# Transposing the probability tiles of two more head pairs by DMA, in attention followed by two feed-forward layers

## The chip, the cores and the metric

The kernel runs on one core of a Trainium2 chip. Its engines are TensorE (PE; its weight loads are listed apart as PEld), VectorE (DVE), ScalarE (ACT), GpSimd (POOL) and SyncE (SP), which here only issues DMAs. The metric is the device time of one execution in microseconds (us).

## What is computed

Attention over 4 batches, 8 heads, 576 positions and 64 channels, with a cut: scores more than tau (0.02) below their row's maximum are dropped. Two feed-forward layers follow on the 2304 tokens.

```
scores = q @ k.T / sqrt(64)
scores = where(scores >= max(scores) - tau, scores, -1e9)
attn = exp(scores - max(scores)); attn /= sum(attn) + 1e-9
x = attn @ v                                   # 2304 x 512
h = ((x @ w1) * (x @ w2)) @ w3 @ w_out         # 1024 wide, back to 512
g = elu(h @ w_in)                              # 2048 wide
out = g @ w_out2                               # 2304 x 512
```

All matmuls keep float32 accuracy. Most operands are split into a high and a low float32r part, and a product is three matmuls (high by high, high by low, low by high).

## The kernel before

**Attention.** The 32 heads are 16 pairs (`NPAIR`); a pair has nine tiles of 128 query rows by 576 keys, so there are 144 tiles, numbered i in the order of `SEQ`. Pairs 0 to 3 ("plain", `NPL = 4`) use unsplit float32 queries and keys. Pairs 4 to 15 use split ones: POOL scales the queries of a head by 1/8 (`prep_s`, L313), ACT makes the high part (`prep_h`, L326), POOL makes the low parts (`prep_lq`, `prep_lk`, L330 and L334).

The path of a tile: PE computes the scores S into a PSUM tile of two banks, of which there are three (`emit_S`, L394 or L406). DVE takes the negated row maximum (`emit_max`, L415). POOL makes a bias for the exponential (`emit_bias`, L423; only for plain tiles and those that a DMA transposes) and then the threshold (`emit_tiny`, L419). ACT takes the exponential (`emit_exp`, L428 or L430). DVE cuts it at the threshold and sums the rows (`emit_mask`, L436). Then P has to be turned so that the keys lie on partitions, in one of two ways:

- On PE: five transposes into the tile's own PSUM banks (`emit_X`, L484) and an ACT copy out of them (`emit_C`, L488). The product with V is then in float32 (`emit_PV`, L541). The PSUM tile stays taken until the copy is done.
- By DMA: ACT rounds P to float16 (`emit_H`, L443), POOL makes the rest that the rounding left (`emit_L`, L447 for 512 columns and L448 for 64), and SP issues a DMA transpose of both (`emit_T`, L474 or L476). The product with V is in float16 (L549). H and L go into a ring of four buffers `hl`, which a DMA transpose frees; the PSUM tile is free after the mask.

Which way a tile goes is said by `of_dma(p, n)`, where n = 0 are the first four tiles of a pair and n = 1 the other five. Before, the n = 0 tiles go by DMA from pair 10 on and the n = 1 tiles from pair 4 on (and of pairs 1 and 3). V in float16 needs a scale for each pair (`v_sum`, `v_mean`, `v_scale`, `prep_v`, `prep_vl`); it is made for every pair from 4 on.

The reciprocals of the row sums of a group (p, n) are made by DVE (`emit_rr`, L496), turned by a PE transpose into unused columns of the PSUM tile of a later score tile (`turn_r`, L502), copied by ACT, stored to DRAM and loaded again as a broadcast. The group's PV waits for that load, and DVE multiplies by it (`emit_xf`).

**First layer, part one.** For a batch of four pairs, both branches x·w1 and x·w2 are computed in units of 8 feature blocks by 2 branches by 2 token groups (`run_ab`, L591; evicted at L599 and L606, and stored to DRAM as g). The units of batches 0 to 2 are planned among the attention tiles, those of batch 3 follow them.

**The planner.** Everything so far is a list of `Op`s with an engine, a duration, dependences and a due time (`key`, mostly the tile number plus a few tiles). `Plan.run` goes through a model of the engines and emits, at each step, among the ops that can begin within `SLACK` of the earliest on an engine, that with the lowest key. `AHEAD` moves the keys by the name of the function and a stage. The result is a fixed instruction order on each engine; nothing is decided on the chip.

**Part two and the second layer** are ordered by hand. w3·w_out is multiplied out first: eight units of 24 matmuls (`m_unit`, L922) into four PSUM banks, each evicted by ACT and DVE (L931, L932) three units later. Among them the next weights are unpacked (L252 to L277: ACT, DVE, DVE, DVE, ACT, POOL for a chunk), and the first block of g is loaded and split (`load_g` L986, `split_g` L241 and L242). Then x2 = M·g (L1125), and the second layer (L1115 to L1280), whose output matmuls (L1206) fill PE to the end.

Of the kernel before, what the change touches and what calls it, by code (L numbers as in the profile page):

```python
# [50 lines left out]
SLACK = {"PE": 0, "DVE": 0.08, "ACT": 0.03, "POOL": 0.27, "SP": 0.09, "NEW": 0.05}  # L51
AHEAD = {
    ("emit_C", 0): 101, ("emit_C", 1): -80.5, ("emit_C", 2): 21, ("emit_H", 1): -14, ("emit_H", 2): 69.5,
    ("emit_L", 2): -5, ("emit_S", 0): 69, ("emit_S", 2): -3.5, ("emit_T", 1): -130, ("emit_T", 2): -16,
    ("emit_X", 0): 3.5, ("emit_X", 2): -0.5, ("emit_bias", 0): 11, ("emit_bias", 1): -33.5, ("emit_bias", 2): -3,
    ("emit_exp", 0): -27.5, ("emit_exp", 1): -18, ("emit_exp", 2): 54.5, ("emit_mask", 0): -37,
    ("emit_mask", 1): -95, ("emit_mask", 2): -18, ("emit_max", 0): -1.5, ("emit_max", 1): -26.5,
    ("emit_max", 2): 17.5, ("emit_rr", 0): -7, ("emit_rr", 1): 36.5, ("emit_tiny", 0): 8, ("emit_tiny", 1): 4,
    ("emit_tiny", 2): -49, ("emit_xf", 0): -88.5, ("emit_xf", 1): -91, ("emit_xh", 0): -44.5, ("emit_xh", 1): 60,
    ("emit_xl", 0): -66.5, ("emit_xl", 1): -29.5, ("evict_a", 0): -25.5, ("evict_a", 1): -24, ("evict_a", 2): 122.5,  # L60
    ("evict_g", 0): -29, ("evict_g", 1): -52, ("evict_g", 2): -1, ("high", 0): -62, ("join", 0): -28.5,
    ("keep_busy", 0): -64, ("keep_r", 0): -22.5, ("keep_r", 1): -20, ("load_plain", 0): 13.5, ("load_qk", 0): 95.5,
    ("load_rs", 0): 39, ("load_rs", 1): 2, ("load_v", 0): 34, ("load_w", 0): -48.5, ("low", 0): 13.5,
    ("new_pt", 0): -58, ("prep_h", 0): -240.5, ("prep_lk", 0): 67, ("prep_lq", 0): -13, ("prep_v", 0): 74,
    ("prep_vl", 0): 21, ("rest", 0): 0.5, ("run_ab", 1): 3, ("run_ab", 2): -4, ("sign", 0): 32.5,
    ("store_g", 0): -98, ("store_g", 1): 93, ("store_g", 2): -149, ("store_r", 0): -12.5, ("store_r", 1): 7,
    ("top", 0): 82, ("turn_r", 0): -155.5, ("turn_r", 1): -142, ("v_mean", 0): -4, ("v_scale", 0): -187,
    ("v_sum", 0): 140.5,
# [8 lines left out]
class Op:  # L77
    def __init__(self, fn, eng, us, key, kb, land, port):
        self.fn, self.eng, self.us, self.key, self.kb, self.land, self.port = fn, eng, us, key, kb, land, port
        self.deps, self.outs, self.n, self.at = [], [], 0, 0.0  # L80
        self.gets = self.frees = None


class Plan:
# [48 lines left out]
    def run(self):  # L133
# [11 lines left out]
        for _ in self.ops:  # L145
# [39 lines left out]
def attention_moe_moe2(  # L185
# [126 lines left out]
    def prep_s(h):  # L312
        G.tensor_scalar(raw[h][:, :S], raw[h][:, :S], esc, 0.0, op0=ALU.mult, op1=ALU.add)  # L313
# [62 lines left out]
    def of_dma(p, n):  # L376
        return p >= 10 if n == 0 else p >= NPL or p % 2 == 1
# [47 lines left out]
    def emit_exp(i):
        et[i] = ep.tile([P, 2, HS], F32, tag="e", name=f"e{i}")
        if i < NPL * TPP:
            A.activation(et[i], sc[i][:, :, :HS], AF.Exp, bias=st[i][:, 2:3], scale=esc)  # L428
        else:
            A.activation(et[i], sc[i][:, :, :HS], AF.Exp, bias=st[i][:, 2:3] if by_dma(i) else st[i][:, 0:1])  # L430

    def emit_mask(i):
        p, pos = SEQ[i]
        if pos == 0:
# [206 lines left out]
    for i in range(NTILE + 4):  # L641
        p, pos = SEQ[i] if i < NTILE else (NPAIR - 1, 0)
        d = 0.02 if i >= NTILE else 1.08 if p < NPL else 1.1 if pos == 8 else 0.58
# [4 lines left out]
        mx = MAX[i] = op(call(emit_max, i), [o], "DVE", 0.672, i)  # L648
# [5 lines left out]
        bi = op(call(emit_bias, i), [mx], "POOL", 0.22, i - 10) if plain or by_dma(i) else mx  # L654
        ty = op(call(emit_tiny, i), [mx, bi], "POOL", 0.24, i - 9)
# [721 lines left out]
```

## Time and profile before

| | us |
|---|---|
| median of three runs | 1008.46 |
| lowest and highest | 1004.95, 1008.83 |
| the profiled execution: its own time | 1006.17 |
| the profiled execution: from first to last instruction | 1004.4 |
| TensorE busy in it | 964.4 (96%) |

The stretches of the profiled execution, in us from its first instruction: attention with tiles 0 to 71 up to about 196, pairs 8 and 9 (tiles 72 to 89) to about 241, pairs 10 to 15 to about 415, the branches of batch 3 to 470, w3·w_out to 518, x2 to 623, the second layer to the end. The chain that ended last can be followed back to 578 us, and nearly all of it is TensorE.

In the windows view a line is a stretch: its length, then for each engine the busy time and the number of instructions, the granted TensorE clock (1.00 is 2.4 GHz, 0.50 is 1.2 GHz), the mean busy share of the 16 DMA engines, and GB/s.

### The profile page before, as it was taken

Reading aid. Unit: us, or ns where it says so; the run is one execution under the profiler, and the core shown is the slowest. Engines: PE = TensorE matmul, PEld = TensorE weight load, DVE = VectorE, ACT = ScalarE, POOL = GpSimd, SP = SyncE. Lnnn points to the kernel's source line nnn. Section 1 sums busy time; section 2 is a strip of 40 time slices with the busy share of each in tenths; the row PEclk is TensorE's granted clock in tenths of the full one; section 3 lists DMA queues with packets and bytes.
Section 4 is the critical chain, followed back from the end, with each engine's and each line's share of the span. In section 5 each row is a group of like instructions: output and inputs, shape, how many; then the busy total and the mean of one; then the engine's idle time right before and its main releaser. Section 6 shows DMA issues by size and latency. Waiting matters only on the chain. (4 is left out here: it accounts for less than half of the span.)

```text
span 1004.4 us, 18071 instructions
## 1 busy us (share of the span) xinstructions
PE 964.4 (96%) x6102; PEld 846.7 (84%) x6102; DVE 716.5 (71%) x1234; ACT 564.2 (56%) x1045; POOL 657.6 (65%) x849
## 2 busy tenths in 40 slices
PE   8899999989999999999999999999999999999998
PEld 5556788858888888899789999898989999899997
DVE  7887988868776677489775654789676656765563
ACT  5787778768666566355435334645555344553442
POOL 4468787868898999255322223888787576875662
PEclk9999999979999999999999999999999999999999
DMA  8446666577887967777747965731215221141201
GB/s 270 152 127 194 135 147 160 143 163 156 190 185 176 191 159 150 192 259 252 250 152 246 311 228 173 260 116 54 65 51 180 72 69 52 49 132 58 69 22 63
DMA packets 182263, 152.51 MB, mean 152 GB/s; under 512 B 119484, under 2 KB 168860, under 8 KB 177564
## 3 DMA queue, kind: packets, MB, share of 16 engines
q1 hardware_dynamic: 178060, 121.72, 44.8%
q10 hardware_dynamic: 4112, 29.66, 8.4%
q8 instruction: 48, 0.79, 0.3%
q14 instruction: 43, 0.35, 0.1%
HBM read 98.89 MB, written 24.72 MB: 123 GB/s over the span
## 5 line engine op out<-in xcount | busy, mean ns | idle before, releaser
L591 PE MATMUL ab<-x,W 128*128 128x256 f32 (+1 forms) x1536 | 227.4, 298 | 0.8 <-DVE xf L560 0.7
L1206 PE MATMUL o<-W,gg 128*128 128x512 f32 x864 | 222.9, 390 | 0.0
L591 PEld LDWEIGHTS ab<-x,W 128*128 128x128 f32 x1536 | 208.3, 188 | 8.2 <-issue 5.2
L1115 POOL TENSOR_TENSOR wi<-wr,wi 128x256 fp32r<-128x256 f32 x168 | 144.3, 871 | 65.8 <-ACT wi L1114 53.3
L1206 PEld LDWEIGHTS o<-W,gg 128*128 128x128 f32 x864 | 159.9, 188 | 21.5
L436 DVE SCALAR_TENSOR_TENSOR e<-s,st,e 128x576 f32<-128x576 f32 x144 | 115.7, 813 | 31.3 <-ACT e L430 24.8
L1194 POOL TENSOR_TENSOR gg<-th,gg 128x384 fp32r<-128x384 f32 x96 | 106.3, 1108 | 46.5 <-PE h L1246 26.4
L415 DVE TENSOR_REDUCE st<-s 128x1 f32<-128x576 f32 x144 | 107.0, 751 | 27.4 <-PE s L406 12.7
L447 POOL TENSOR_TENSOR hl<-e,hl 128x512 f16<-128x512 f32 x94 | 110.4, 1175 | 19.7 <-ACT hl L443 19.2
L1246 PE MATMUL h<-sl,wi 128*128 128x384 f32 x576 | 116.5, 338 | 2.1 <-DVE th L1276 1.2
L1188 ACT ACTIVATE et<-et 128x384 f32<-128x384 f32 x96 | 50.1, 522 | 111.9 <-DVE et L1187 111.5
L1246 PEld LDWEIGHTS h<-sl,wi 128*128 128x128 f32 x576 | 102.5, 188 | 11.2 <-DVE th L1276 2.0
L1125 PE MATMUL x<-sl,M 128*128 128x384 f32 x576 | 100.6, 336 | 1.4 <-DVE sl L242 1.4
L1125 PEld LDWEIGHTS x<-sl,M 128*128 128x128 f32 x576 | 99.8, 188 | 2.1 <-DVE sl L242 2.0
L1193 ACT ACTIVATE gg<-th 128x384 fp32r<-128x384 f32 x96 | 50.6, 527 | 76.9 <-DVE th L1191 76.5
L1276 DVE TENSOR_TENSOR th<-h,th 128x384 f32<-128x384 f32 x96 | 53.2, 554 | 56.9 <-PE h L1246 56.8
L406 PE MATMUL s<-qk 128*128 128x288 f32 x480 | 86.7, 310 | 7.1 <-DVE e L436 3.7
L430 ACT ACTIVATE e<-s,st 128x576 f32<-128x576 f32 x108 | 77.8, 736 | 27.1 <-POOL st L423 21.5
L1246 PE MATMUL h<-so,wi 128*128 128x384 f32 x432 | 87.5, 337 | 2.6 <-ACT th L1286 1.8
L1246 PEld LDWEIGHTS h<-so,wi 128*128 128x128 f32 x432 | 76.6, 188 | 10.8 <-ACT th L1286 3.9
L406 PEld LDWEIGHTS s<-qk 128*128 128x128 f32 x480 | 69.5, 192 | 17.0 <-issue 6.2
L1191 DVE SCALAR_TENSOR_TENSOR th<-et,th 128x384 f32<-128x384 f32 x96 | 71.6, 746 | 16.8 <-ACT et L1188 15.4
(112 smaller groups left out, 1539.0 us busy)
## 6 DMA issues: line engine op xcount, KB each, us to landing
wr<-wi_dr SPq DMA_DIRECT2D x168, 128.0 KB
rqk<-in_qk SPq DMA_DIRECT2D x24, 576.0 KB
raw_wo<-in_wo ACTq DMA_DIRECT2D x12, 1024.0 KB
th<-g_dr SPq DMA_DIRECT2D x48, 192.0 KB
raw_w<-in_w SPq DMA_DIRECT2D x8, 1024.0 KB
raw_w<-in_w3t ACTq DMA_DIRECT2D x8, 1024.0 KB
raw_win<-in_win ACTq DMA_DIRECT2D x8, 1024.0 KB
vr<-in_v SPq DMA_DIRECT2D x16, 320.0 KB
```

The lines of the kernel that those rows point to most:

```text
L406: T.matmul(s[:, n, :HS], q, k[:, c:c + HS], start=(x == 0), stop=(x == len(ops) - 1))
L415: V.tensor_reduce(st[i][:, 0:1], sc[i][:, :, :HS], axis=AX.XY, op=ALU.max, negate=True)
L430: A.activation(et[i], sc[i][:, :, :HS], AF.Exp, bias=st[i][:, 2:3] if by_dma(i) else st[i][:, 0:1])
L436: V.scalar_tensor_tensor(et[i], sc[i][:, :, :HS], st[i][:, 1:2], et[i], op0=ALU.is_ge, op1=ALU.mult, accum_out=sm[p][:, pos:pos + 1],)
L447: G.tensor_tensor(t[:, S + 64:], e[:, :512], t[:, :512], op=ALU.subtract)
L591: T.matmul(o[:, :w], wf[:, m, wx, kt, :], x[:, xx, :], start=(kt == 0 and k == 0), stop=(kt == NK - 1 and k == 2),)
L1115: G.tensor_tensor(t[:, 1], r, f32(t[:, 0]), op=ALU.subtract)
L1125: T.matmul(o[:, :TB], M[:, f, mx, e * P:(e + 1) * P], gh[j, f][:, gx, :], start=(k == 0), stop=(k == 23),)
L1191: V.scalar_tensor_tensor(x, c["t"], -1.0, x, op0=ALU.add, op1=ALU.max)
L1194: G.tensor_tensor(h[:, 1, :], x, f32(h[:, 0, :]), op=ALU.subtract)
L1206: T.matmul(po[j, t], dst["h"][:, gx, t * P:(t + 1) * P], WO[f][:, wx, :], start=(first and k == 0), stop=(last and k == 2),)
L1246: T.matmul(o[:, :TB], w[:, wx, kt, :], bs[k][:, kt, xx, :], start=(i == 0), stop=(i == 5),)
```

## The change

- `of_dma`: the n = 0 tiles go by DMA from pair 8 on. These are eight tiles, four each of pairs 8 and 9.
- Scores of pairs 4 to 15 are computed negated (`prep_s` multiplies by `nesc`), the row maximum becomes a minimum, and the mask compares with `is_le`. Thereby threshold and bias are both a sum with the same minimum, and one POOL instruction writes them side by side (`emit_tiny`); `emit_bias` is left for plain tiles alone.
- `turn_r` uses the PSUM tile of q + 3, not q + 2.
- In the stage of w3·w_out, `load_g` is issued after the first four units, two at a time, and `split_g` starts after the fourth unit, not after the first.
- The planner: new durations, new `SLACK`, a rule that PE's writes into a PSUM tile and the other engines' reads of it don't overlap (`bank`, `wr`), and an `AHEAD` of 377 entries, by groups of twelve tiles or two pairs, where there were 74. The order on every engine is thus new up to 470 us.

```diff
-SLACK = {"PE": 0, "DVE": 0.08, "ACT": 0.03, "POOL": 0.27, "SP": 0.09, "NEW": 0.05}
+SLACK = {"PE": 0.0, "DVE": 0.07, "ACT": 0.06, "POOL": 0.35, "SP": 0.0, "NEW": 0.05}
...
+        if o.bank in self.touched[not o.wr]:
+            t = max(t, self.touched[not o.wr][o.bank] + LAT)
...
+            if o.bank is not None:
+                self.touched[o.wr][o.bank] = end
...
     def prep_s(h):
-        G.tensor_scalar(raw[h][:, :S], raw[h][:, :S], esc, 0.0, op0=ALU.mult, op1=ALU.add)
+        G.tensor_scalar(raw[h][:, :S], raw[h][:, :S], nesc, 0.0, op0=ALU.mult, op1=ALU.add)
...
     def of_dma(p, n):
-        return p >= 10 if n == 0 else p >= NPL or p % 2 == 1
+        return p >= 8 if n == 0 else p >= NPL or p % 2 == 1
...
+        plain = SEQ[i][0] < NPL
-        V.tensor_reduce(st[i][:, 0:1], sc[i][:, :, :HS], axis=AX.XY, op=ALU.max, negate=True)
+        V.tensor_reduce(st[i][:, 0:1], sc[i][:, :, :HS], axis=AX.XY, op=ALU.max if plain else ALU.min, negate=plain)
...
     def emit_tiny(i):
         t = st[i]
-        G.tensor_scalar(t[:, 1:2], t[:, 0:1], -1.0, add2[:, (k := int(i >= NPL * TPP)):k + 1], op0=ALU.mult, op1=ALU.add)
+        if SEQ[i][0] < NPL:
+            G.tensor_scalar(t[:, 1:2], t[:, 0:1], -1.0, add2, op0=ALU.mult, op1=ALU.add)
+            return
+        w = 1 + by_dma(i)
+        G.tensor_tensor(t[:, 1:1 + w], lift[:, :w], t[:, 0:1].to_broadcast([P, w]), op=ALU.add)
...
-        i = q + 2
+        i = q + 3
-        tr = op(call(turn_r, p, n, i), [r, S_[i]], "PE", 0.11, q)
+        tr = op(call(turn_r, p, n, i), [r, S_[i]], "PE", 0.08, q, bank=i, wr=True)
...
+    def next_g(f):
+        split_g(0, f)
+        load_g(JS[1], f)
+
-    for f in range(NF1):
-        load_g(JS[0], f)
     for f in range(NF1):
         while jobs and f not in w3s:
             run_jobs(1)
         run_unit(m_unit(f), 2)
+        if f < 4:
+            load_g(JS[0], 2 * f)
+            load_g(JS[0], 2 * f + 1)
         if f < 6:
             run_jobs(4)
-        split_g(0, f)
-        load_g(JS[1], f)
+        if f > 2:
+            next_g(f - 3)
+    for f in range(NF1 - 3, NF1):
+        next_g(f)
     flush(0)
```

## Rows read from the trace of the kernel before

**Rows 1.** The page: busy us and share of the span of each engine.

```profile
PE 964.4 (96%) x6102; PEld 846.7 (84%) x6102; DVE 716.5 (71%) x1234; ACT 564.2 (56%) x1045; POOL 657.6 (65%) x849
```

**Rows 2.** The windows view, by stretches (columns as told above).

```profile
0.00:196.00 196.00, 184.91 (x1398) 138.06 (x1399) 164.70 (x337) 145.92 (x230) 137.79 (x232) 1.00 0.61 168
196.00:241.00 45.00, 40.71 (x284) 31.52 (x285) 34.33 (x75) 32.11 (x55) 33.30 (x53) 0.89 0.66 151
241.00:415.00 174.00, 163.45 (x1374) 150.69 (x1369) 123.03 (x272) 112.72 (x199) 148.89 (x260) 1.00 0.81 174
250.00:350.00 100.00, 94.03 (x762) 86.17 (x761) 69.94 (x155) 64.29 (x113) 87.20 (x149) 1.00 0.85 187
470.40:518.36 47.96, 45.47 (x195) 37.11 (x194) 39.02 (x36) 20.11 (x28) 17.11 (x7) 0.96 0.64 226
623.00:1004.40 381.40, 373.28 (x1860) 334.43 (x1859) 253.46 (x396) 182.07 (x413) 267.61 (x270) 1.00 0.28 89
```

**Rows 3.** Waits of PE, whole span: total us, times, longest.

```profile
PE s L502 <- DVE st L415: 5.2, 7, 1.7
...
PE m L922 <- DVE M L932: 2.5, 1, 2.5
...
PE s L502 <- DVE rr L497: 2.1, 3, 0.9
```

**Rows 4.** Timeline of SP at 202 us: start, us, what.

```profile
202.47 6.19 SPq L476 DMA_TRANSPOSE pt<-hl  x4
```

**Rows 5.** Timeline of ACT there; in brackets the idle time before, and its releaser.

```profile
207.00 0.68 ACT L443 ACTIVATE hl<-e 128x576 f16<-128x576 f32 x1 [2.13 <-DMA pt<-hl]
```

**Rows 6.** Timeline of PE there.

```profile
201.88 0.77 PE L484 MATMUL s<-ident,e 128*128 128x128 f32 x5
202.58 1.08 PE L541 MATMUL pv<-pt,vr 128*64 128x256 f32 x8
...
208.33 2.82 PE L406 MATMUL s<-qk 128*128 128x288 f32 x12 [1.68 <-ACT pt L488]
...
213.84 1.33 PE L406 MATMUL s<-qk 128*128 128x288 f32 x4 [0.58 <-ACT pt L488]
```

**Rows 7.** Groups of PE, whole span: busy us, mean ns of one, idle before.

```profile
L484 PE MATMUL s<-ident,e 128*128 128x128 f32 x200 | 32.0, 283 | 3.3 <-DVE e L436 3.2
...
L541 PE MATMUL pv<-pt,vr 128*64 128x256 f32 x160 | 20.5, 387 | 0.0
L484 PE MATMUL s<-ident,e 128*64 128x128 f32 x50 | 13.8, 276 | 0.0
L549 PE MATMUL pv<-pt,v 128*64 128x256 f16 x168 | 10.5, 274 | 2.0 <-ACT a L599 2.0
L541 PE MATMUL pv<-pt,vr 64*64 64x256 f32 x40 | 6.5, 402 | 0.0
```

**Rows 8.** Groups of POOL from 241 to 409 us.

```profile
L447 POOL TENSOR_TENSOR hl<-e,hl 128x512 f16<-128x512 f32 x57 | 67.1, 1177 | 5.8 <-ACT hl L443 5.4
L448 POOL TENSOR_TENSOR hl<-e,hl 128x64 f16<-128x64 f32 x57 | 19.3, 338 | 0.0
L419 POOL TENSOR_SCALAR st<-st,add 128x1 f32<-128x1 f32 x57 | 18.0, 316 | 5.3
...
L423 POOL TENSOR_SCALAR st<-st 128x1 f32<-128x1 f32 x57 | 12.0, 210 | 6.8 <-DVE st L415 1.6 <-ACT hl L443 0.6
```

**Rows 9.** Timeline of PE in the stage of w3·w_out.

```profile
470.40 21.94 PE L922 MATMUL m<-WO,w 128*128 128x512 f32 x96
494.83 23.69 PE L922 MATMUL m<-WO,w 128*128 128x512 f32 x96 [2.49 <-DVE M L932]
```

**Rows 10.** Timeline of ACT there.

```profile
482.61 0.53 ACT L241 ACTIVATE sl<-th 128x384 fp32r<-128x384 f32 x1 [7.68 <-DMA th<-g_dr]
```

**Rows 11.** Timeline of DVE there.

```profile
483.18 0.56 DVE L242 TENSOR_TENSOR sl<-th,sl 128x384 fp32r<-128x384 f32 x1 [4.83 <-ACT sl L241]
...
494.10 0.68 DVE L932 TENSOR_TENSOR M<-m,M 128x512 fp32r<-128x512 f32 x1
```

More of the change, by code (lines that the diff above doesn't have):

```diff
@@ L50 @@
 LAT = 0.06
-SLACK = {"PE": 0, "DVE": 0.08, "ACT": 0.03, "POOL": 0.27, "SP": 0.09, "NEW": 0.05}
+SLACK = {"PE": 0.0, "DVE": 0.07, "ACT": 0.06, "POOL": 0.35, "SP": 0.0, "NEW": 0.05}
 AHEAD = {
[L53 to L68, printed above, removed]
@@ new lines @@
+    ("emit_C", 0, 0): 184, ("emit_C", 0, 1): 178.5, ("emit_C", 1, 1): -20.5, ("emit_C", 1, 2): -196,
+    ("emit_C", 2, 3): -74, ("emit_C", 2, 4): -72, ("emit_C", 2, 5): -80.5, ("emit_H", 1, 1): -29,
+    ("emit_H", 1, 2): -20.5, ("emit_H", 2, 3): 710.5, ("emit_H", 2, 4): 791.5, ("emit_H", 2, 5): 1038,
+    ("emit_H", 2, 6): 966.5, ("emit_H", 2, 7): 845, ("emit_H", 2, 8): 797.5, ("emit_H", 2, 9): 835,
+    ("emit_H", 2, 10): 836, ("emit_H", 2, 11): 763.5, ("emit_L", 1, 1): -179.5, ("emit_L", 1, 2): 17,
@@ L647, in attention_moe_moe2 @@
             continue
-        mx = MAX[i] = op(call(emit_max, i), [o], "DVE", 0.672, i)
+        mx = MAX[i] = op(call(emit_max, i), [o], "DVE", 0.672, i, bank=i)
         rs = take("st", 6, mx)
@@ L653, in attention_moe_moe2 @@
         plain = p < NPL
-        bi = op(call(emit_bias, i), [mx], "POOL", 0.22, i - 10) if plain or by_dma(i) else mx
-        ty = op(call(emit_tiny, i), [mx, bi], "POOL", 0.24, i - 9)
-        ex = op(call(emit_exp, i), [bi], "ACT", 0.715 if plain else 0.625, i)
+        if plain:
+            bi = op(call(emit_bias, i), [mx], "POOL", 0.25, i - 10)
+            ty = op(call(emit_tiny, i), [mx, bi], "POOL", 0.25, i - 9)
+        else:
+            ty = op(call(emit_tiny, i), [mx], "POOL", 0.27, i - 9)
+            bi = ty if by_dma(i) else mx
+        ex = op(call(emit_exp, i), [bi], "ACT", 0.73 if plain else 0.645, i, bank=i)
         re = take("e", EB, ex)
-        mk = MASK[i] = op(call(emit_mask, i), [ex, ty], "DVE", 0.79, i - 2)
+        mk = MASK[i] = op(call(emit_mask, i), [ex, ty], "DVE", 0.75, i - 2, bank=i)
         if pos == 0:
@@ L665, in attention_moe_moe2 @@
         if by_dma(i):
-            hi = op(call(emit_H, i), [mk], "ACT", 0.575, i - 1)
+            hi = op(call(emit_H, i), [mk], "ACT", 0.6, i - 1)
             rh = take("hl", HLB, hi)
-            lo = op(call(emit_L, i), [hi], "POOL", 1.42, i - 1)
+            lo = op(call(emit_L, i), [hi], "POOL", 1.44, i - 1)
             re += [mk, hi, lo]
@@ L672, in attention_moe_moe2 @@
         else:
-            xo = op(call(emit_X, i), [mk], "PE", 0.54, i - 2)
-            co = op(call(emit_C, i), [xo], "ACT", 0.59, i - 3)
+            xo = op(call(emit_X, i), [mk], "PE", 0.61, i - 2, bank=i, wr=True)
+            co = op(call(emit_C, i), [xo], "ACT", 0.61, i - 3, bank=i)
             ring["s", i] += [xo, co]
```

151 lines of the change are left out of this document (121 added, 30 removed).

## The prediction

> **What bounds the kernel now.** First the page. TensorE is busy 96% of the span [rows 1], so what a change can win is TensorE work, TensorE's idle time, or time at the lower clock. Then the windows by stretches [rows 2], which say where those are. In the last 381.4 us, the second layer, PE idles 8.1 us, and the change doesn't touch it. In attention PE idles 11.1 us up to 196 us, 4.3 us in pairs 8 and 9 (196 to 241), and 10.6 us in pairs 10 to 15 (241 to 415). In pairs 8 and 9 the granted clock is 0.89, a loss of 0.11 x 45 = 5.0 us more: a stretch at 1.2 GHz of twice that length. In the stage of w3·w_out PE idles 2.5 us, and the clock, 0.96 on average, takes 0.04 x 48 = 1.9 us.
>
> In pairs 10 to 15 two more resources are nearly full: POOL with 148.9 of 174 us (86%), and the DMA engines with a share of 0.81. TensorE is filled up there with the branch units of batches 1 and 2. So PE, POOL and DMA have to be reckoned for 196 to 415 us together. That stretch lasts 219 us now.
>
> What happened in pairs 8 and 9 is told by three timelines. SP took 6.19 us for four transposes, 1.55 us each [rows 4]. ACT, whose order is fixed, stood 2.13 us before an `emit_H` until a transpose gave a buffer of `hl` free [rows 5]. Queued behind that H were the copies `emit_C` that free PSUM tiles; the next scores waited for them, 1.68 us and once more 0.58 us [rows 6]. After that the clock fell to 1.2 GHz. It is thus the mixture of both ways of turning P in one pair that made this stall.
>
> **The change part by part.**
>
> *TensorE work removed.* Eight tiles lose `emit_X`. Five transposes start 0.70 us before the next instruction [rows 6], while the groups give (32.0 + 13.8) / 50 = 0.92 us a tile [rows 7]. I take 0.70, as starts count on a pipelined engine: 5.6 us, at most 7.3. Two groups n = 0 have PV in float16: (20.5 + 6.5) / 10 = 2.70 us against 10.5 / 6 = 1.75 us a group, 1.9 us for both. Sum: 7.5 us, at most 9.2. V in float16 is made for these pairs anyway and costs nothing more.
>
> *The stall.* With no `emit_C` left in pairs 8 and 9, a late H doesn't hold a PSUM tile there any more. The clock loss of 5.0 us and the waits of 1.68 and 0.58 us go: 7.2 us, if nothing like it comes up elsewhere.
>
> *POOL.* Added in pairs 8 and 9: eight `emit_L` of 1.18 + 0.34 us [rows 8], 12.1 us. Removed: the bias instruction of 0.21 us for each DMA tile from pair 8 on, 10 in pairs 8 and 9 (2.1 us) and 54 in pairs 10 to 15 (11.3 us). The fused instruction isn't in the trace. From below: `emit_L` costs 1177 ns for 512 columns and 338 for 64, which leaves an estimated 0.22 us at no columns. From above: 0.316 + 0.210 = 0.53 us, that is, nothing saved. I take the 0.316 us of `emit_tiny`, the nearest in size and place. POOL then needs 33.3 + 12.1 - 2.1 = 43.3 us in pairs 8 and 9, and 148.9 - 11.3 = 137.6 us in pairs 10 to 15. That load makes pairs 8 and 9 slower in themselves. PE doesn't stand meanwhile, as branch units of batch 1 are there to fill in; without them the 10 us more of POOL would show in full.
>
> *Both together, 196 to 415 us.* PE sets one limit: 204.2 us busy [rows 2], less 5.0 for the clock and 7.5 removed, is 191.7. With the idle time that is left, 14.9 - 2.3 = 12.6 us, it is 204.3 us. POOL sets another: 43.3 + 137.6 = 180.9 us of work. The share that it has held over 100 us of attention is 0.872 [rows 2], and at that share it takes 207.5 us. The two limits are 204 and 207 us, near enough to hinder one another by turns; I take a little above both, 208.5 us. Gain: 10.5 us. The bounds of the fused instruction, 72 times -0.10 to +0.21 us, move POOL's limit to 200 or to 225 us.
>
> *A rule against the PE limit.* PE was busy 93% of these 219 us, its weight loads 83% (31.5 + 150.7 us) [rows 2]. The Trainium skill, "Perfetto Trace Analysis", section "Identifying the Most-Contended Engine", holds that matmul busy time is no measure of headroom, and that the share of weight loads is one of the good ones. By that, PE isn't the limit here, removing its work gains nothing by itself, and the stretch would be POOL's 207.5 us, 1 us less than in my sum, and rival B below would fall out. The trace agrees in part only: in the second layer weight loads are at 88% too, and PE is at 98% with the chain of the end lying on it.
>
> *Reciprocals one tile later.* `turn_r` waited 5.2 us for a maximum that was reading its PSUM tile, and 2.1 us for the reciprocal [rows 3]. A later tile and the planner's new rule address both. What it is moved past: on PE one tile's scores, and with it the copy on ACT, the store and the load on SP and the PV that waits for them come up to a tile (174 / 54 = 3.2 us) later. PV's lateness is hidden by branch units; at the very end of attention, where there are none, it would cost 3.2 us once. What of the gain lies in 196 to 415 us is inside POOL's limit already. For 0 to 196 us I take 1 us, between +3.2 and -5.2 - 2.1 = -7.3.
>
> *The stage of w3·w_out.* ACT stood 7.68 us before the first split of g, because the load hadn't landed [rows 10]; DVE then stood 4.83 us for ACT [rows 11]. All weight unpacking was queued behind. The first eviction of M came at 494.10 us, and PE, with its four banks full after 96 matmuls in 21.94 us, waited 2.49 us [rows 9]. In the new order the splits come behind that eviction. It loses the 4.83 us and three splits of 0.55 us ahead of it: 494.1 - 6.5 = 487.6 us, and PE needs the bank at 492.3. The wait and the low clock behind it go, 2.5 + 1.9 = 4.4 us. The loads of g go past nothing on SP, as it has only these in the stage. The three splits that now come last need 3 x 0.55 us, beside the last unit of 21.94 / 4 = 5.5 us. If that cover were gone, the stall would stay: bounds 0 and -4.4.
>
> *Without effect:* minimum for maximum, `is_le`, the negated scores (same instructions, sizes and engines), the branches of batch 3 and all after 518 us, which follow PE.
>
> **Sum**, against the profiled execution's own 1006.2 us: -10.5 - 1 - 4.4 = -15.9, that is 990 us. This execution lies 2.3 us under the median of 1008.5 and inside the runs' spread of 1005 to 1009, so I add nothing for that.
>
> **The rivals.**
>
> *PE sets the pace* (B). POOL runs at 0.91, and the new order halves PE's remaining 12.6 us: 191.7 + 6.3 = 198 us, a gain of 21. With 2 and 4.4 us it is 979 us. For it: up to 196 us PE idles only 6%, start included. Against: POOL's 0.87 in [rows 2] would have to rise while it also has pairs 8 and 9 to carry.
>
> *DMA sets the pace* (C). Pairs 8 and 9 had a DMA time of 0.66 x 45 = 29.7 us, pairs 10 to 15 had 140.9, in sum 170.6. A transpose adds between 1.55 us [rows 4] and, from the difference of the pairs, (140.9 / 6 - 29.7 / 2) / 4 = 2.2 us. With 1.75, near the direct row, eight are 14 us: 184.6. The highest share over 100 us of attention is 0.85 [rows 2]: 217 us, a gain of only 2. With 1 and 4.4 us that is 999 us. For it: 184.6 / 208.5 is 0.885, more than was ever reached there. Against: at 0.85 PE was still 94% busy and at full clock [rows 2].
>
> *Slower: transposes hold up H* (D). The share of DMA falls, as eight more transposes meet the loads of queries and keys and the H behind them stand in ACT's order ahead of everything, as in [rows 5]. At 0.79 the stretch is 184.6 / 0.79 = 234 us, 15 us longer than now; less 5.4 it is 1016 us. It is slower by over 0.5% from 232 us, a share of 0.796, against 0.81 in pairs 10 to 15. Against: those pairs have all nine tiles by DMA and no fall of the clock.
>
> *The order doesn't do what it says* (E). The new plan has the removed stall and a second one like it elsewhere, 7.2 us each: 990.3 + 14.4 = 1005 us; or one such stall, and the stage of w3·w_out keeps its wait: 1002 us. Nearly no change.
>
> **How the numbers follow.** Forecast, 984 to 995 us: 0.47. B 0.15, C 0.18, E 0.12, D 0.08. A measurement of this kernel can tell about 0.5% from no change, that is 5 us; faster means under 1003.4, slower over 1013.5. The forecast, B, C and a bit of E give faster 0.82; the rest of E and a part of D no change, 0.11; slower 0.07. The range leaves out the lower part of B and the upper of E and D: 977 to 1003 us.
>
> **What would show each step.** In the new trace: no L488 and L484 for the eight tiles; granted clock 1.00 from 196 to the end of attention, which comes near 403 us; a fused POOL instruction of 0.3 us; POOL at 0.87 or more in pairs 8 to 15 (forecast), DMA at 0.85 with H waiting for transposes (C); waits at L502 under 3 us; no wait at L922, eight units in 43.9 us at clock 1.00, x2 starting some 15.9 us earlier than 518.4. The prediction is wrong if the clock falls again in attention, if the fused instruction takes over 0.5 us, or if H stands before transposes for longer than now.

## The result, and the profile after

The changed kernel takes 1019.0 us (median of 5, 1018.0 to 1026.1), the kernel before 1008.5 us beside it. These two medians are 10.6 us apart; the recorded ratio is 1.0148, 95% interval 1.0114 to 1.0181, which is some 15 us, and the medians of before in the later series, 1004.6 to 1006.0 us, bear that out. So the changed kernel is slower, where 990 us were forecast, and outside the range. The profiled execution is the longest of its five, 1026.1 us.

The page of after (its engines' line; then two groups: line, engine, tiles, form, count | busy us, mean ns | idle us before them and its releasers):

```profile
PE 973.4 (95%) x6078; PEld 850.6 (83%) x6078; DVE 725.5 (71%) x1235; ACT 563.0 (55%) x1045; POOL 637.6 (62%) x781
...
L490 PE MATMUL s<-qk 128*128 128x288 f32 x480 | 86.2, 311 | 15.7 <-DVE e L524 14.5
...
L531 ACT ACTIVATE hl<-e 128x576 f16<-128x576 f32 x102 | 67.9, 678 | 47.6 <-DMA pt<-hl 35.4
```

L490 are the scores, which wait for masks (`emit_mask`, L524), and L531 is `emit_H`, which waits for transposes to give its buffer free. Both waits stand again in the views of PE and of ACT (total us, times, longest), up to the stage of w3·w_out:

```profile
PE s L490 <- DVE e L524: 14.5, 9, 6.7
PE pv L637 <- DMA pt<-hl: 7.4, 7, 3.1
...
PE pv L637 <- DMA rb<-rd: 2.6, 1, 2.6
```

```profile
ACT hl L531 <- DMA pt<-hl: 35.4, 27, 3.0
```

Before, the same wait of H was a third of that:

```profile
ACT hl L443 <- DMA pt<-hl: 12.1, 8, 2.6
```

The windows of after (first 72 tiles; pairs 8 and 9; pairs 10 to 15; what of the branch units is left; stage of w3·w_out; second layer):

```profile
0.00:204.00 204.00, 189.73 (x1396) 140.09 (x1397) 169.95 (x338) 146.51 (x231) 128.71 (x214) 0.98 0.63 164
204.00:262.00 58.00, 45.18 (x325) 36.64 (x325) 41.06 (x87) 35.10 (x61) 42.19 (x66) 0.88 0.77 159
262.00:422.00 160.00, 146.22 (x1189) 133.70 (x1188) 118.05 (x250) 103.87 (x182) 125.88 (x193) 0.98 0.88 173
422.00:489.30 67.30, 66.56 (x536) 65.14 (x535) 47.96 (x58) 30.03 (x45) 27.57 (x15) 1.00 0.79 241
489.30:532.79 43.49, 43.49 (x194) 36.01 (x193) 37.51 (x36) 19.87 (x27) 16.07 (x7) 1.00 0.70 246
636.00:1024.30 388.30, 380.27 (x1873) 337.73 (x1872) 252.18 (x397) 184.51 (x417) 267.52 (x270) 1.00 0.28 88
```

The bounds of [rows 2] at 241 and 415 us are not the same points of the work: counted by the masks, they lie some 5 us before and 6 us behind those of 262 and 422 us in after. So here is before at the same points, and the line that [rows 2] lacks:

```profile
196.00:246.00 50.00, 45.71 (x328) 36.07 (x328) 38.60 (x83) 36.24 (x62) 37.73 (x60) 0.90 0.64 149
246.00:409.00 163.00, 152.75 (x1265) 140.76 (x1263) 117.21 (x259) 106.84 (x189) 143.02 (x251) 1.00 0.82 177
409.00:470.40 61.40, 59.36 (x474) 58.42 (x475) 44.29 (x52) 27.54 (x41) 24.66 (x11) 1.00 0.76 244
415.00:470.40 55.40, 53.66 (x415) 53.05 (x414) 42.75 (x47) 25.78 (x36) 23.22 (x9) 1.00 0.74 256
```

Attention ends at 489.3 us instead of 470.4 [rows 9]: 18.9 us lost. By these points the first 72 tiles take 204 us instead of 196, pairs 8 and 9 58 instead of 50, pairs 10 to 15 160 instead of 163, and the branch units that are left 67.3 instead of 61.4. (In e17, the same program with one tile longer, attention ended at 484.2, and in e12, another order of it, at 482.9; the loss in a usual execution is nearer to these.) The stage of w3·w_out takes 43.5 instead of 48.0 us, 4.5 won. x2 takes 103.2 instead of 101.8 us, 1.4 lost. The second layer takes 388.3 us; before, from its first matmul of h at 620.2 to the end, it was 384.2: 4.1 us lost.

For attention I split the time into PE's work (busy time, less the share of the clock that was missing times the length) and what PE lost (idle time and clock). Before: 184.91 + 40.71 + 163.45 + 53.66 - 0.11 x 45 = 437.8 of 470.4, so 32.6 lost. After: 447.7 - 0.02 x 204 - 0.12 x 58 - 0.02 x 160 = 433.4 of 489.3, so 55.9 lost. The work fell, as it should; what PE lost rose by 23 us.

Where the largest single loss arose is told by the timelines around 210 to 222 us, the passage from pair 7 to pair 8. ACT from one exp to the next (copies without a long wait left out):

```profile
209.63 0.72 ACT L518 ACTIVATE e<-s,st 128x576 f32<-128x576 f32 x1
...
213.47 0.83 ACT L443 ACTIVATE v<-vr,vst 128x640 f16<-128x640 f32 x1 [2.05 <-DVE vst L439]
...
216.44 0.68 ACT L531 ACTIVATE hl<-e 128x576 f16<-128x576 f32 x1 [1.32 <-DMA pt<-hl]
218.37 0.68 ACT L531 ACTIVATE hl<-e 128x576 f16<-128x576 f32 x1 [1.24 <-DMA pt<-hl]
219.31 0.68 ACT L531 ACTIVATE hl<-e 128x576 f16<-128x576 f32 x1 [0.26 <-DMA pt<-hl]
219.90 0.72 ACT L518 ACTIVATE e<-s,st 128x576 f32<-128x576 f32 x1
```

SP, DVE and PE there:

```profile
210.93 5.83 SPq L564 DMA_TRANSPOSE pt<-hl  x3
```

```profile
220.65 0.82 DVE L524 SCALAR_TENSOR_TENSOR e<-s,st,e 128x576 f32<-128x576 f32 x1 [3.80 <-ACT e L518]
```

```profile
207.32 0.68 PE L679 MATMUL ab<-x,W 128*128 128x320 f32 x3
...
221.62 1.30 PE L490 MATMUL s<-qk 128*128 128x288 f32 x4 [6.69 <-DVE e L524]
...
239.23 2.03 PE L679 MATMUL ab<-x,W 128*128 128x320 f32 x12
```

Three transposes of pair 7 took SP 5.83 us. Three H (the last of pair 7, the first two of pair 8) wait for them on ACT, and the exp stands behind these H in ACT's fixed order: there is none between 209.63 and 219.90. So the mask is late, the PSUM tile stays taken, and PE waits 6.69 us. In this window the granted clock is 0.88, a loss of 7 us through stretches at 1.2 GHz. PE had nothing to fill in with: no branch unit (L679) ran from 208 to 239 us, 31 us. Before, there was such a gap too, but of 24 us:

```profile
199.01 0.60 PE L591 MATMUL ab<-x,W 128*128 128x320 f32 x3
...
223.26 0.60 PE L591 MATMUL ab<-x,W 128*128 128x320 f32 x3
```

### The profile page after: what moved, and what is told of

Its sections match the earlier page's. It is cut to its first block, busy times and chain, and to the rows that moved or that the text cites. A ratio compares the mean times of both kernels' runs of the same rounds, so it can differ in the third digit from the quotient of the medians.

```text
span 1024.3 us, 17843 instructions
## 1 busy us (share of the span) xinstructions
PE 973.4 (95%) x6078; PEld 850.6 (83%) x6078; DVE 725.5 (71%) x1235; ACT 563.0 (55%) x1045; POOL 637.6 (62%) x781
## 4 chain that ended last, share of the span: by engine, by line
PE 54%; DVE 4%; DMA 3%; POOL 3%; issue 2%; ACT 1%; SPq 0%; ACTq 0%; DVEq 0%; POOLq 0%
PE o L1306 17%; PE h L1346 15%; PE x L1225 9%; PE ab L679 7%; PE m L1015 4%; DVE th L1291 1%; POOL hl L535 1%; PE pv L637 1%; DMA pt<-hl 1%; DVE et L1287 1%; DMA x_dr<-x2s 0%; DVE th L1376 0%; DMA rqk<-in_qk 0%; POOL hl L536 0%; POOL qk L418 0%
## 5 line engine op out<-in xcount | busy, mean ns | idle before, releaser
L679 PE MATMUL ab<-x,W 128*128 128x256 f32 (+1 forms) x1536 | 226.6, 298 | 2.4 <-DVE g L694 1.4
L1306 PE MATMUL o<-W,gg 128*128 128x512 f32 x864 | 226.5, 394 | 0.0
L679 PEld LDWEIGHTS ab<-x,W 128*128 128x128 f32 x1536 | 208.9, 188 | 11.2 <-issue 4.5
L535 POOL TENSOR_TENSOR hl<-e,hl 128x512 f16<-128x512 f32 x102 | 120.5, 1181 | 34.9 <-ACT hl L531 31.1
L524 DVE SCALAR_TENSOR_TENSOR e<-s,st,e 128x576 f32<-128x576 f32 x144 | 115.8, 812 | 36.1 <-ACT e L518 34.1
L490 PE MATMUL s<-qk 128*128 128x288 f32 x480 | 86.2, 311 | 15.7 <-DVE e L524 14.5
L531 ACT ACTIVATE hl<-e 128x576 f16<-128x576 f32 x102 | 67.9, 678 | 47.6 <-DMA pt<-hl 35.4
L490 PEld LDWEIGHTS s<-qk 128*128 128x128 f32 x480 | 69.4, 192 | 25.2 <-issue 14.6
L518 ACT ACTIVATE e<-s,st 128x576 f32<-128x576 f32 x108 | 78.1, 733 | 14.7 <-POOL st L508 10.8
```

What stands on the lines that cost most here:

```text
L490: T.matmul(s[:, n, :HS], q, k[:, c:c + HS], start=(x == 0), stop=(x == len(ops) - 1))
L524: V.scalar_tensor_tensor(et[i], sc[i][:, :, :HS], st[i][:, 1:2], et[i], op0=ALU.is_ge if p < NPL else ALU.is_le, op1=ALU.mult, accum_out=s ...
L531: A.activation(hl[i][:, :S], et[i].rearrange("p a b -> p (a b)"), AF.Copy)
L535: G.tensor_tensor(t[:, S + 64:], e[:, :512], t[:, :512], op=ALU.subtract)
L679: T.matmul(o[:, :w], wf[:, m, wx, kt, :], x[:, xx, :], start=(kt == 0 and k == 0), stop=(kt == NK - 1 and k == 2),)
L1306: T.matmul(po[j, t], dst["h"][:, gx, t * P:(t + 1) * P], WO[f][:, wx, :], start=(first and k == 0), stop=(last and k == 2),)
```

## The experiments

Ratios are to the kernel before on the same chip, with 95% intervals. Each edit names the kernel, before or after, that it alters.

### The parts alone

**e1**, before with the new stage of w3·w_out only:

```diff
-    for f in range(NF1): load_g(JS[0], f)
...
+        if f > 2: next_g(f - 3)
```

> The kernel before, with only the later loads and splits of g in the stage of w3·w_out. Both theories expect the same here: the wait of 2.5 us at L922 and the stretch at 1.2 GHz behind it go, 4.4 us: 1004 us, a ratio of 0.996. The stage of w3·w_out lasts 43.5 us, not 48.0. If the gain is given back later (x2 waiting for its splits), the ratio is 1.000.

Measured 1002.4 us, ratio 0.9978 [0.9957, 0.9999]. In its profile the stage takes 43.6 us and the clock doesn't fall. The gain is just clear of noise and smaller than the profile's 4.4 us: the old stage doesn't stall in every execution (in e6 and e15 it took 43.6 and 43.8 us with the old code).

**e6**, before with negated scores and the fused instruction, in the order of before:

```diff
-        G.tensor_scalar(t[:, 1:2], t[:, 0:1], -1.0, add2[...], ...)
+        G.tensor_tensor(t[:, 1:1 + w], lift[:, :w], t[:, 0:1].to_broadcast([P, w]), op=ALU.add)
```

> The kernel before, with negated scores and the fused threshold and bias put where the bias stood; every other instruction keeps its place on its engine. If the fused instruction is harmless, POOL loses about 20 us of work in the whole, and the time is 1000 to 1005 us, a ratio of 0.995 to 1.000. If it is itself a cause of the loss (the exponential waiting for a longer instruction), the ratio is 1.004 or more.

Measured 1006.6 us, ratio 1.0024 [0.9998, 1.0049]. POOL's share between 241 and 409 us fell from 0.88 to 0.79 (147.5 to 132.1 of 168 us), and attention ended at 469.9 us (before 470.4). So POOL's work wasn't what set the pace there.

**e2**, before with the eight tiles by DMA only, ordered by its own planner:

```diff
-        return p >= 10 if n == 0 else p >= NPL or p % 2 == 1
+        return p >= 8 if n == 0 else p >= NPL or p % 2 == 1
```

> The kernel before, with only the eight tiles of pairs 8 and 9 by DMA; planner, its durations and due times as before. Theory H (more transposes make ACT stand before H, H holds up the exponentials, and so PE's scores): ACT's wait before H rises from 12 to 25 us or more, and the time to 1015 us or more. Theory N (it is the new order, not the eight tiles): PE loses 7.5 us of work, H waits stay under 15 us, and the time is 998 to 1004 us.

Measured 1026.7 us, ratio 1.0197 [1.0154, 1.0240]: this edit, with the order that the old planner then makes, costs 20 us. H waits 21.2 us and the scores 14.7 us for masks, 7.2 us the longest, as in after:

```profile
ACT hl L443 <- DMA pt<-hl: 21.2, 16, 3.0
...
PE s L406 <- DVE e L436: 14.7, 12, 7.2
```

### The order

**e3**, after without the eight tiles (`p >= 10` again), **e8**, after with the due times, the `SLACK` and no PSUM rule as before, **e12**, after with `LAT = 0.061` for 0.06, and **e5**, before with the same:

```diff
-        return p >= 8 if n == 0 else p >= NPL or p % 2 == 1
+        return p >= 10 if n == 0 else p >= NPL or p % 2 == 1
...
-LAT = 0.06
+LAT = 0.061
```

> The kernel after, with the eight tiles back on PE; the new planner with all its due times, the fused instruction, the later reciprocals and the new stage of w3·w_out stay. Theory H: ACT's wait before H falls from 35 to 15 us or less, and the time to 1005 us or less. Theory N: H waits stay over 25 us, and the time stays at 1015 us or more.

> The kernel after with all its program changes and its durations, but SLACK, AHEAD with its stages, and the rule on PSUM tiles as before. If the new due times and rule are worse than the old ones, it is faster than 1016 us. If they did mend most of what the eight tiles cost (theory: the new due times are fitted to the new list), it is slower than 1022 us.

> The changed kernel with nothing but the planner's latency constant at 0.061 instead of 0.060 us: another order of the same instructions. Theory 1 (the eight tiles' list costs the time, whichever way it is ordered): 1014 to 1024 us, H waits 25 us or more in all. Theory 2 (this one order is a bad one): it moves by more than 5 us, below 1014 or over 1024, with H's waits moving the same way.

> The kernel before, with one number of the planner's model changed by a nanosecond (a hop between engines 0.061, not 0.060 us). Nothing is computed otherwise, and the same instructions run; only their order on the engines before 470 us comes out another way. Theory R (the due times were fitted to one order, and any new order loses that): 1012 us or more. Theory S (orders of this planner are much alike): within 4 us of 1005 us, so that the losses of the runs before belong to the eight tiles and to the new due times.

Measured: e3 1.0121 [1.0086, 1.0156], e8 1.0246 [1.0214, 1.0278], e12 1.0147 [1.0104, 1.0191], e5 1.0078 [1.0050, 1.0105]. Another order of after's instructions gives the same time (e12), so after isn't one unlucky order. The new due times and rule win back about 1% of the time (e8 against after). But an order of before that differs by nothing real costs 0.8% (e5), and the new order without the eight tiles 1.2% (e3):

```profile
ACT hl L531 <- DMA pt<-hl: 29.6, 25, 3.9
```

So both runs that leave the order of before pay for it, with H waiting little longer in e5 (13.0 us) and much longer in e3. How much another order would cost on average isn't known from one shuffle of each kernel.

### One more buffer for H

**e4**, after with five buffers of `hl` instead of four (room for it by multiplying `xf` in place), and **e7**, before with the same:

```diff
-    hlp = sa.enter_context(tc.tile_pool(name="hlp", bufs=HLB))
+    hlp = sa.enter_context(tc.tile_pool(name="hlp", bufs=5))
...
-        xf[p, n] = f = rbp.tile([P, 320], F32, tag="xf", name=f"xf{p}_{n}")
+        xf[p, n] = f = rbc[p, n]
```

> The kernel after, in the very same order on every engine, with five buffers for H and L instead of four (their room is won by multiplying the reciprocals in place, which drops the two buffers of xf). Theory H: with one buffer more, ACT's wait before H falls from 35 us to 20 or less, the 6.7 us wait of PE for a mask goes, and the time falls by 6 us or more, to 1013 us or less. Theory C (the DMA engines themselves are the limit): the waits move elsewhere and the time stays within 3 us of 1019 us. Theory N (the order is bad in other ways): H waits fall but PE still waits for masks, time within 4 us of 1019 us.

> The kernel before in its own order, with five buffers for H and L instead of four (xf in place). Theory H: ACT's wait before H falls from 12 to 4 us or less, the stall at 206 us and the stretch at 1.2 GHz behind it go, and the time falls by 5 to 8 us, to 997 to 1000 us. If H waits don't reach PE, it stays within 2 us of 1005 us.

Measured: e4 1015.6 us, 1.0112 [1.0066, 1.0158]; e7 1002.8 us, 0.9973 [0.9953, 0.9992]. In e4, the waits of the scores and of H, and the window of pairs 10 to 15:

```profile
PE s L490 <- DVE e L524: 10.4, 6, 5.5
...
ACT hl L531 <- DMA pt<-hl: 9.5, 6, 4.3
```

```profile
255.00:409.00 154.00, 142.91 (x1185) 132.14 (x1183) 115.58 (x250) 102.72 (x181) 126.03 (x194) 0.99 0.93 180
```

H waits a quarter of its 35.4 us, and the DMA engines are busy to 0.93 instead of 0.88. So their rate wasn't the limit in after; the buffers were a part of it. But the time falls by 3.4 us only, and the intervals overlap: PE still waits 5.5 us for a mask at the passage, where the two H of pair 8 still stand before transposes (0.55 and 1.15 us) and the exp behind them. In e7, H waits 1.9 us instead of 12.1, the wait of 1.68 us for copies [rows 6] is gone (one of 0.50 stands), and the granted clock from 196 to 241 us is 0.96 instead of 0.89, with both ways of turning P still mixed in pairs 8 and 9. The gain of 2.7 us is half of the 5 to 8 expected.

### The transposes left out

**e9** (pairs 8 and 9), **e10** (8 to 15), **e13** (7), **e14** (7 to 15) of after, and **e15** (10 to 15) of before, each with its own order:

```diff
     def emit_T(i):
         p, pos = SEQ[i]
+        if p >= 8:
+            return
...
-                x_ = q[:, c, j, :w // D if p < NPL else w]
+                x_ = v16[p][:, j, x, :w] if p >= 8 else q[:, c, j, :w // D if p < NPL else w]
```

> The changed kernel with its own list and order, but the 18 transposes of pairs 8 and 9 are left out (all of both pairs), and their PV multiplies by an array of V of the same shape instead of P: part of the computation is left out, the rest of TensorE, ACT, DVE and POOL does the same instructions. Theory 1, the transposes in flight cost the time (H stands before them, masks come late, the clock falls): the 13.9 us that H waits in pairs 8 and 9 go, PE's idle time plus clock loss there falls from 19.6 us to about 5, and the time from 1019 to 1003 to 1007 us. Theory 2, the list and its new order cost it: PE's idle time there stays over 12 us and the time is 1013 us or more.

> The same for pairs 8 to 15: none of the changed kernel's 72 tiles is transposed by DMA, and PV reads an array of V in place of P (that part of the computation is left out). Theory 1: H waits for nothing, no fall of the clock from 204 us to the end of attention, PE's idle time plus clock loss before the stage of w3 w_out falls from 55 us to about 25, time 985 to 992 us, which would be the forecast's 990 without transposes in the way. Theory 2: H waits nothing, but masks, POOL and PE still hold one another up: idle time plus clock loss 40 us or more, time over 1004 us.

> The kernel before in its own order, without the 54 tiles' transposes of pairs 10 to 15 (PV reads an array of V there; that part is left out). If its transposes cost it as much as they cost the changed kernel (15 us): about 991 us, and the changed list is worse even with none in flight. If they cost it only what shows as waits (H 9.4 us, PE idle 10.3 us in pairs 10 to 15): 998 to 1002 us, and the changed kernel without them (1003.7) is as good within 5 us.

> The changed kernel in its own order, with only the five transposes of pair 7 left out (its second PV multiplies by an array of V in place of P; that part of the computation is left out). Theory 3, the passage: H of pair 8 stands behind these five on ACT, ahead of the exp whose mask frees the PSUM tile. Then PE's wait of 6.7 us at 221 us and the 10 us at the low clock go, branch units of batch 1 start before 232 us instead of 239, and the time falls by 8 to 12 us, to 1008 to 1012 us; H's waits in pairs 10 to 15 stay at about 20 us. If the order alone makes the stall: PE still waits over 4 us there and the time is 1015 us or more.

> The same for pairs 7 to 15, all transposes behind pair 6 left out. Theory 3: what e10 kept in pairs 8 and 9 (9.5 us idle and 6.8 us of clock) falls to about 6 in all, the time from 1003.7 to 993 to 997 us. Order alone: 1001 us or more.

Measured: e9 1012.1 us, 1.0071 [1.0047, 1.0096]; e10 1003.7 us, 0.9984 [0.9960, 1.0008]; e15 997.0 us, 0.9933 [0.9910, 0.9956]; e13 1013.5 us, 1.0093 [1.0056, 1.0130]; e14 1000.0 us, 0.9943 [0.9921, 0.9965]. Windows of e10, then of e15 (first 72 tiles; pairs 8 and 9; 10 to 15; rest of the branch units):

```profile
0.00:200.00 200.00, 186.38 (x1396) 138.15 (x1397) 167.84 (x338) 146.47 (x231) 128.87 (x214) 1.00 0.65 167
200.00:253.00 53.00, 43.53 (x323) 35.96 (x323) 39.90 (x85) 35.99 (x62) 41.40 (x65) 0.87 0.41 104
253.00:398.60 145.60, 140.92 (x1193) 130.79 (x1192) 119.38 (x252) 103.96 (x182) 126.62 (x195) 1.00 0.26 81
398.60:465.60 67.00, 66.26 (x533) 64.83 (x532) 47.50 (x58) 29.45 (x45) 27.08 (x14) 1.00 0.64 216
```

```profile
0.00:197.30 197.30, 186.94 (x1403) 139.20 (x1404) 164.34 (x339) 146.40 (x232) 137.46 (x233) 1.00 0.61 167
197.30:247.30 50.00, 45.06 (x326) 35.88 (x325) 38.19 (x82) 35.83 (x62) 37.28 (x60) 0.90 0.65 146
247.30:405.50 158.20, 151.48 (x1263) 140.25 (x1261) 116.16 (x260) 107.70 (x189) 142.42 (x251) 1.00 0.30 85
405.50:465.40 59.90, 59.07 (x475) 58.02 (x476) 44.13 (x51) 27.36 (x41) 24.62 (x11) 1.00 0.70 239
```

Two readings. First, without its transposes in pairs 8 to 15 the changed kernel gains 1.0148 - 0.9984 = 1.6%, 16 us, and the kernel before, without those in pairs 10 to 15, 0.7%, 7 us. (In the profiles, 4.2 us of what e15 gains are the stall in the stage of w3·w_out, which doesn't come in every execution.) What e10 still takes longer than e15 lies behind attention: x2 takes 1.4 and the second layer 4.9 us more. Second, e10 isn't at its forecast of 985 to 992 us. Its PE work is 430.2 us (437.1 less 0.13 x 53) against 437.5 in e15, the 7.3 us that the change removes; and still attention ends at 465.6 us in one and 465.4 in the other. With no transpose of pairs 8 to 15 in the way, e10 loses 35.4 us and e15 27.9. Pairs 8 and 9 lie among that: 9.5 us idle and 6.9 of clock, against 4.9 and 5.0. e9 says the same: without the transposes of pairs 8 and 9 the time is 1012, not the 1003 to 1007 us of theory 1.

That is the passage again, since the transposes of pair 7 are still there. PE in e10, then in e13 and in e14:

```profile
217.27 1.30 PE L490 MATMUL s<-qk 128*128 128x288 f32 x4 [6.36 <-DVE e L524]
...
233.34 2.03 PE L681 MATMUL ab<-x,W 128*128 128x320 f32 x12
```

```profile
214.84 1.30 PE L490 MATMUL s<-qk 128*128 128x288 f32 x4 [4.06 <-DVE e L524]
...
228.18 2.03 PE L681 MATMUL ab<-x,W 128*128 128x320 f32 x12
```

```profile
215.17 1.30 PE L490 MATMUL s<-qk 128*128 128x288 f32 x4 [4.15 <-DVE e L524]
...
228.45 2.03 PE L681 MATMUL ab<-x,W 128*128 128x320 f32 x12
```

Leaving out pair 7's five transposes alone (e13) wins back 0.55%, hardly more than the noise of the two intervals together; the wait at the passage falls from 6.7 to 4.1 us and branch units start at 228 instead of 239 us. Theory 3 is right for a part: the other 4.1 us stand with no transpose of pairs 7 to 15 at all (e14). There ACT still has V's scaling (L443, 2.1 us behind DVE) and three H ahead of the exp, and no branch unit is left. That this order makes the rest of the wait is read from the timeline; no run moves the exp ahead of the H.

What PE lost, idle time and clock together, can be told by stage, with bounds at the same points of the work in each trace (to some 2 us). In us:

| | first 72 tiles | pairs 8 and 9 | pairs 10 to 15 | rest | sum |
|---|---|---|---|---|---|
| before | 11.1 | 9.3 | 10.2 | 2.0 | 32.6 |
| after | 18.4 | 19.8 | 17.0 | 0.7 | 55.9 |
| e17, after with a pad | 14.9 | 17.9 | 16.0 | 0.7 | 49.5 |
| e3, after, eight tiles on PE | 13.9 | 9.3 | 17.2 | 0.8 | 41.2 |
| e13, after, no transposes of 7 | 13.3 | 11.4 | 17.2 | 0.7 | 42.6 |
| e10, after, none of 8 to 15 | 13.6 | 16.4 | 4.7 | 0.7 | 35.4 |
| e14, after, none of 7 to 15 | 13.6 | 9.7 | 6.2 | 0.7 | 30.2 |
| e15, before, none of 10 to 15 | 10.4 | 9.9 | 6.7 | 0.8 | 27.9 |

The excess at the passage, some 8 us, goes from either side: with the eight tiles back on PE (e3, which has an order of its own), or without pair 7's transposes (e13, e14). So it takes both, the H of pair 8 and the transposes ahead of them; the 4.1 us wait that is left costs no more than what before loses there. The excess in pairs 10 to 15, 6 to 7 us, is in e3 too: the new order brings it, not the eight tiles, and it goes with the transposes there. The first 72 tiles lose 13 us or more in every kernel with after's list and durations (e8 too) and 10 to 12 in all others; which part of the list does it, no run tells.

### The second layer

Its matmul of 512 columns by 128 rows (`o`), from 640 to 980 us, in before, e16, e6, after and e17:

```profile
L1206 PE MATMUL o<-W,gg 128*128 128x512 f32 x781 | 202.5, 390 | 0.0
```

```profile
L1213 PE MATMUL o<-W,gg 128*128 128x512 f32 x782 | 202.8, 390 | 0.0
```

```profile
L1221 PE MATMUL o<-W,gg 128*128 128x512 f32 x772 | 203.6, 394 | 0.0
```

```profile
L1306 PE MATMUL o<-W,gg 128*128 128x512 f32 x754 | 198.9, 394 | 0.0
```

```profile
L1306 PE MATMUL o<-W,gg 128*128 128x512 f32 x766 | 201.4, 393 | 0.0
```

Eleven profiled kernels had the negated scores, the fused instruction and its two constants without a pad: there `o` takes 394 ns and the layer 388.1 to 388.8 us. Six had none of these (before, e1, e5, e7, e15, e16), and e2 neither: 390 ns, and 383.9 to 384.6 us. e6 shows that this part alone brings it. The matmuls of 512 columns in the stage of w3·w_out don't share it: 389 ns in e6 and after, as in e7 and e16. I supposed that it is the place of the tiles in SBUF, which the new constants push on by 64 bytes. **e17**, after, and **e18**, e11 below, make it 128 bytes:

```diff
-    lift = cst.tile([P, 2], F32, name="lift")
+    lift = cst.tile([P, 24], F32, name="lift")
```

> The changed kernel with one number altered: the tile of the new constants is 24 values long instead of 2, so that all later SBUF tiles lie 128 bytes a partition behind where the kernel before has them, instead of 64. Order and instructions are the same. If the place of the tiles slows the matmuls: the second layer takes 384.2 us instead of 388.3, its matmul of 512 columns 390 ns instead of 394, and the time falls by 4 to 5.5 us, ratio to before 1.009 to 1.011 instead of 1.0148. If not (the number of instructions, or chance): 388 us and 394 ns as they were, ratio 1.013 to 1.017.

Measured 1019.2 us, ratio 1.0151 [1.0122, 1.0179], 393 ns, layer 387.6 us; in e18 both come out the same. The place has some effect (0.7 us), and it isn't the cause of the 4.1 us, or not in this simple form. The cause stays open.

### A version that beats both?

**e11**, before with e1's stage, e7's buffers and e6's instruction; **e16**, the same without e6's; **e18**, e11 with the pad.

> A version of its own: the kernel before in its own list and order, with the three things that gained or were free by themselves: the new loads and splits of g in the stage of w3 w_out (ratio 0.9978 alone), a fifth buffer for hl with xf multiplied in place (0.9973 alone), and the fused threshold and bias (1.0024 alone). If the gains add up: 0.995 to 0.9975, that is 1000 to 1002.5 us against 1005. If they fall on the same idle time: 0.9975 to 1.000. If the fused instruction costs what it cost alone: 0.9975.

> A version of its own: the kernel before with the new loads and splits of g in the stage of w3 w_out and a fifth buffer for hl, without the fused instruction. If the gains add up: 0.993 to 0.9965 (999 to 1002.5 us against 1006). If not: 0.9965 to 0.999, as with the fused instruction (0.9977).

> e11 (the kernel before in its order, with the new stage of w3 w_out, five buffers of hl and the fused instruction) with the same pad. If the place of the tiles is the cause: second layer 384.2 us instead of 388.4, ratio 0.992 to 0.995 instead of 0.9977. If not: 0.996 to 0.999.

Measured: 0.9977 [0.9953, 1.0001], 0.9990 [0.9968, 1.0011], 0.9995 [0.9976, 1.0014]. The two gains seen alone (e1, e7) don't add up, and no version that computes everything is faster than the kernel before by more than 0.5%. All three beat the changed kernel by over 14 us.

## Why the prediction was wrong, step by step

- **TensorE work removed: right.** 7.5 us forecast; 7.3 from e15 to e10, 4.4 from before to after (437.8 to 433.4). Over all profiles PE's work up to the end of attention is 437 to 442 us in the ten kernels with the eight tiles on PE and 430 to 435 in the ten with them by DMA.
- **The stall: the step that failed.** "With no `emit_C` left in pairs 8 and 9, a late H doesn't hold a PSUM tile there any more." It did, by another way: H stands ahead of the exp on ACT, and it is the mask behind the exp that frees the tile. I had followed only the copies out of [rows 5, 6] and not what else is queued behind an H. Instead of 7.2 us won, pairs 8 and 9 lost 12.8 us idle and 7.0 of clock, against 4.3 and 5.0 before. e3 and e13 show from two sides that the H of pair 8 behind the transposes of pair 7 made the excess (9.3 and 11.4 us there, 17.9 in e17). That is as much as the removed work was worth: e3, without the eight tiles, is about as fast as after.
- **The cover: failed.** "Branch units of batch 1 are there to fill in." They weren't: they start when pair 7's attention is through, at 239 us. In the trace of before, too, none ran from 199.6 to 223.3 us, around the very stall of [rows 6]; I hadn't read there when a batch's first unit can run.
- **POOL and Both together: failed.** For 196 to 415 us a gain of 10.5 us was forecast; at the same points of the work pairs 8 to 15 took 213 us before and 218 after. The share of 0.872 was a result, not a limit: it rose to 142.42 / 158.2 = 0.90 in e15, and fell to 125.88 / 160 = 0.79 in after, in a stretch only 3 us shorter than before. e6 took 9 points off it for nothing. The fused instruction itself was cheaper than the 0.316 us that I took, near the lower bound; POOL's group from 204 to 425 us:

```profile
L508 POOL TENSOR_TENSOR st<-lift,st 128x2 f32<-128x2 f32 x73 | 17.2, 241 | 18.3 <-DVE st L500 17.0 <-DVE rr L584 0.7
```

- **The rule against the PE limit: not settled.** From it I drew that removing PE's work gains nothing by itself. e10 has 7.3 us less of that work than e15, and attention ends at 465.6 us in one and 465.4 in the other; but e10 also loses 6.5 us more at the passage and 3.2 more in the first 72 tiles, so the work can have been won and lost again. The rule itself is that of the Trainium skill, "Perfetto Trace Analysis", section "Identifying the Most-Contended Engine", that matmul busy time is no good measure of how near TensorE is to its limit; no run here shows it. What took POOL's place in my reading was no engine's share, but waits.
- **Reciprocals: half right.** `turn_r` waits 0.6 us for the maximum instead of 5.2 [rows 3]. In the profile of after a PV waited 2.6 us for its load, near the step's price of up to 3.2 us, but inside attention, where I had thought it covered; in e17 and e12 none did. The 1 us that I took for 0 to 196 us didn't come: that stretch lost 2 to 4 us more in most profiles, 7 in that of after. The later tile was never run alone, so its own part is open.
- **The stage of w3·w_out: right** in the profile, 4.5 us and no wait; as a mean over executions worth 2.2 us (e1).
- **Without effect: failed.** The second layer is 4.1 us longer, put at nothing in the sum; e6 ties it to the fused instruction and its constants. Nothing in the trace of before pointed to it.
- **The rivals.** D had the mechanism (H ahead of everything in ACT's order), with 0.08 far too low; its own argument against, that pairs 10 to 15 were already all by DMA without a fall of the clock, took the buffers' slack there for granted. Its way of reckoning failed too: the share over pairs 8 to 15 was 185.5 / 218 = 0.85, not 0.79. C's figures look met: its 184.6 us of DMA time are 0.77 x 58 + 0.88 x 160 = 185.5, and its 217 us for the stretch were 218. That is luck, as before has 213 us and 0.64 x 50 + 0.82 x 163 = 165.7 us of DMA time at these points, not 219 and 170.6. And e4 ran the DMA engines at 0.93, so their share was no limit either. E had a stall elsewhere, which the new order did bring (pairs 10 to 15), but a net time near that of before. B forecast a gain of 27 us, and nothing in the traces bears it out. And no rival had the first 72 tiles 8 us later (5 in e17), the branch units that were left over for the end (67 us instead of 61), or the second layer.

The sum of attention, worked out for one pair of profiles: 4.4 us of work won; 23.3 more lost. 20.5 us less are lost in e10, but 4.8 of these lie in the first 72 tiles, before any transpose that e10 leaves out: they belong to this execution of after. With e17 in its place, 3.1 us of work are won and 16.9 more lost: some 4 in the first 72 tiles, 8.6 at the passage, 6 in pairs 10 to 15, less 1.3 in the rest. Without any transposes in pairs 8 to 15 the changed kernel loses 7.5 us more than before without its own (e15): 6.5 at the passage, none of them without the transposes of pair 7 (e14), and 3.2 in the first 72 tiles, less 2 won in pairs 10 to 15.

## What to carry to other kernels

On an engine whose order is written by hand, list everything that is queued behind an instruction before you say what its wait costs, and follow each item to the buffer that it frees; one wait can hold the same PSUM tile in two ways. A resource's highest share so far is not its limit: leave its work out in one run, and see whether the stretch gets shorter. And where work is "filled in", look up in the trace from when on the filler can run at all.

## What the runs showed of the hardware that I had not expected

- One matmul, of the same form and operands, took 390 or 394 ns throughout a kernel, in the same way in every kernel with the fused instruction and its two constants, which run 200 us and more earlier; that is 4 us of the whole. A pad of SBUF moved it to 393. Its cause is not found.
- A POOL instruction that writes two values from two tiles took 0.24 us, one that writes one value with a constant multiplied and a tile added 0.32 [rows 8]: the number of values did not set the cost.
- The DMA engines were busy to 0.93 over 154 us (e4) once H had a buffer more, above the 0.85 that I had taken for their highest.
- From after to e10, pairs 10 to 15 have 15.8 MB of traffic less (27.4 to 11.6) and 104 us less of the DMA engines' time (0.876 x 160 to 0.251 x 145.6). By this estimate the transposes moved 153 GB/s at full share, and the rest of the traffic 318.
